# Softmax attention and a Mish feed-forward on one core: three attention outputs in a row in place of one beside each half step

## The chip, the core and the metric

The kernel runs on one core of a Trainium2 chip. A core has engines with instruction queues of their own, which run side by side and wait for one another through semaphores: TensorE (PE: matmuls, and transposes as matmuls), VectorE (DVE), ScalarE (ACT: exponentials, Mish, copies), GpSimd (POOL) and the DMA queues that SyncE (SP) and POOL feed. Each engine takes its instructions strictly in the order in which the program gives them. Matmul results land in PSUM, eight banks of 128 x 512 fp32 values; everything else on the chip lies in SBUF. The metric is the device time of one execution in microseconds.

## The reference

Attention over q, k, v of shape (8, 12, 448, 64), whose softmax has one extra term in the denominator, then a feed-forward with Mish on the (3584, 768) result:

```python
scores = scale * np.matmul(q, k.transpose(0, 1, 3, 2))
m = np.max(scores, axis=-1, keepdims=True)
e = np.exp(scores - m)
attn = e / (np.sum(e, axis=-1, keepdims=True) + np.exp(-m) + 1e-09)
x = np.matmul(attn, v)                       # -> (B*S, H*D) = (3584, 768)
h = x @ w_in                                 # (768, 2048)
g = h * np.tanh(np.log1p(np.exp(h)))         # Mish; for h > 20 the softplus is h
out = g @ w_out                              # (2048, 768)
```

Inputs and output are fp32; inside, the kernel multiplies bf16 and adds up in fp32.

## The kernel before, in words

**Pairs, units and batches.** Two heads make a pair (48 pairs, 6 to a batch), three pairs make a unit, two units a batch. The first batch (pairs 0 to 5) goes through a loop of its own. From then on the program is a loop over units u = 2 to 19 (L525): units 2 to 15 have attention, 16 to 19 are the tail with feed-forward work alone. Instructions are issued in the order of the source (`manual_schedule`, L51), so the loops are the plan of every engine's queue.

**The twelve steps of a unit (L536).** A pair has four steps. Steps 0, 1 and 2 of a pair handle two tiles of 128 query rows each; step 3 handles one and is called the half step. (A unit's steps are n = 0 to 11; 3, 7 and 11 are the half steps.) Step n does this:

- `exps` (L274): ACT takes the exponential of the scores of step n, one activation per tile, with row sums into `sums`, and so frees a scores tile.
- `flush_late` (L102): DVE makes the copies out of PSUM that were put off: of an attention output to xT (L366) or of the output product to o_sb (L422).
- Output product (`mm2_part`, L406): PE multiplies a share of the unit's pieces, of a row of products that are ready to be made for an earlier pair of batches (L456 to L471). A quarter piece is 192 columns over two of the 16 inner tiles; a unit has 56 (unit 4 has 40). `weight` (L474) says how much of it each step takes.
- `scores_ahead` (L221): PE multiplies the scores of step n + 3 into the tile just freed, and DVE takes the row maxima (L269, `negm`), which the exponential needs as its bias.

There are three scores tiles, `sc0` to `sc2`, each of two PSUM banks (L71); step n uses tile n mod 3. A half step uses only the first bank of its tile. Two more single-bank tiles, `mo0` and `mo1`, serve the output product and the in-projection in turn.

**The attention output (`av_pair`, L343).** For each pair 8 matmuls multiply the normalised, transposed exponentials eT by v; each has 64 output rows, and the two heads go to the two halves of a bank. `av_with` (L533) ties the three pairs of the unit before to the half steps of this unit: when the scores of a half step are issued, the attention output is multiplied first, into the second bank of the same scores tile (L242). Half steps are issued three steps ahead, so this falls at steps 0, 4 and 8, and each copy to xT at steps 1, 5 and 9.

**The second part of a unit (L577).** After the twelve steps come eight groups of the in-projection (`mm1_mish`, L374): 6 matmuls over the six 128-row slices of xT (L381), then Mish on ACT (L387) to gT. The third group uses the first bank of `sc0`, the others `mo` tiles. In even units these are the first eight groups of a batch and use the attention outputs that were multiplied in the same unit; in odd units they are the last eight, whose xT has been complete for a unit, while the outputs just multiplied belong to the next batch. Between the groups DVE makes the denominators (L295, L299) and normalises the exponentials (L316; the third pair on POOL, L314), SP transposes them by DMA into eT (L320), and the next unit's q and k are transposed on PE (L178), copied out (L209, L217), and its first three scores multiplied.

Of the kernel before, what the change touches and what calls it, by code (L numbers as in the profile page):

```python
# [15 lines left out]
UNIT_PAIRS = 3  # L16
# [3 lines left out]
def kernel(  # L20
# [28 lines left out]
    STEPS = 4  # L49
# [3 lines left out]
    def pool(name, bufs, space=None):  # L53
# [17 lines left out]
    sc_tiles = [  # L71
        psum.tile([128, 2, 512], FP32, tag=f"sc{i}", name=f"sc{i}") for i in range(3)
    ]
# [22 lines left out]
    ]  # L96

    loaded, casted, qkT, att, xT, gT, o_sbs, stats = {}, {}, {}, {}, {}, {}, {}, {}
    av_with = {}
    late = deque()  # L100

    def flush_late():  # L102
        while late:
            late.popleft()()

    def mo_take():

        if not mo_free:
            flush_late()
        return mo_free.popleft()  # L110
# [110 lines left out]
    def scores_ahead(limit):  # L221

        while rg["next"] < limit and rg["used"] < len(sc_tiles):
            rg["used"] += 1
            scores(rg["next"])
            rg["next"] += 1

    def scores(idx):

        p, s = divmod(idx, STEPS)  # L230
        if s == 0:
            if p < HP or p % UNIT_PAIRS == 0:
                for nm in ("negm", "sums", "expm", "den", "rden"):
                    stats[nm] = st_pool.tile([128, UNIT_PAIRS, NTILE], FP32, tag=nm, name=nm)
            at = 0 if p < HP else p % UNIT_PAIRS
            att[p] = {nm: t[:, at, :] for nm, t in stats.items()}
            att[p].update(en=en_bufs[p % N_EN], whole=dict(stats))
        st = att[p]
        qT, kT = qkT[p]
        kA, kB = kT[0:64, :], kT[64:128, :]  # L240
        sc = sc_tiles[idx % len(sc_tiles)]
        if s == STEPS - 1 and p in av_with:  # L242
            av_pair(av_with.pop(p), bank=sc[:, 1, :])
        if p >= DIAG_FROM:
            cols = tuple(range(2 * s, min(2 * s + 2, NTILE)))
            negm = st["negm"][:, cols[0] : cols[-1] + 1]
            for bk, i in enumerate(cols):
                nc.tensor.matmul(  # L248
                    sc[:, bk, 0:S], lhsT=qT[:, i].rearrange("d h r -> d (h r)"), rhs=kT,
                    start=True, stop=True,  # L250
                )
        elif s < 3:
            qa, qb = 128 * s, 64 + 128 * s
            nc.tensor.matmul(  # L254
                sc[:, 0, 0:S], lhsT=qT[0:64, qa : qa + 128], rhs=kA, start=True, stop=True
            )
            nc.tensor.matmul(
                sc[:, 1, 0:S], lhsT=qT[64:128, qb : qb + 128], rhs=kB, start=True, stop=True
            )
            cols, negm = (s, 4 + s), st["negm"][:, s : s + 5 : 4]  # L260
        else:
            nc.tensor.matmul(
                sc[0:64, 0, 0:S], lhsT=qT[0:64, 384:S], rhs=kA, start=True, stop=True
            )
            nc.tensor.matmul(
                sc[64:128, 0, 0:S], lhsT=qT[64:128, 0:64], rhs=kB, start=True, stop=True
            )
            cols, negm = (3,), st["negm"][:, 3:4]
        nc.vector.tensor_reduce(  # L269
            out=negm, in_=sc[:, 0 : len(cols), 0:S], axis=AX.X, op=ALU.max, negate=True  # L270
        )
        st["sc", s] = (sc, cols)
# [70 lines left out]
    def av_pair(p, act=False, bank=None):  # L343
        b, hp = p // HP, p % HP
        eT = att[p]["eT"]
        v_bf = casted[p][2]
        if b not in xT:
            xT[b] = xT_pool.tile([128, DM_T, S], BF16, tag="xT", name="xT")
        av = mo_take() if bank is None else bank
        for j in range(NT):  # L350
            for h in range(2):
                if p >= DIAG_FROM:
                    by_h = eT[0:SP_, j, :].rearrange("c (i h r) -> c h i r", h=2, r=64)
                    e_h = by_h[:, h]
                else:
                    e_h = eT[0:SP_, j, h * S : (h + 1) * S]
                nc.tensor.matmul(  # L357
                    av[h * 64 : (h + 1) * 64, 0:S],
                    lhsT=v_bf[:, h, j * D : (j + 1) * D],
                    rhs=e_h,  # L360
                    start=(j == 0), stop=(j == NT - 1),
                )
        copy = nc.scalar.copy if act else nc.vector.tensor_copy

        def evac():
            copy(out=xT[b][:, hp, :], in_=av[:, 0:S])  # L366
            if bank is None:
                mo_free.append(av)

        late.append(evac)  # L370
        del att[p], casted[p], qkT[p]
# [76 lines left out]
    steps = UNIT_PAIRS * STEPS  # L448
    first_mm2 = 2 * UNITS_PER_B
# [22 lines left out]


    weight = [5.2] + [1.0] * (steps - STEPS) + [0.4] * (STEPS - 1)  # L474

    LEAD = UNIT_PAIRS + 1
    LOAD_AT = (0, 3, 6)
# [47 lines left out]
    for u in range(UNITS_PER_B, N_UNITS + 2 * UNITS_PER_B):  # L525
        attn = u < N_UNITS
        filler = deque()
        for part in plan.get(u, []):
            filler.extend(mm2_part(*part))
        total, done, acc = sum(w for _, w in filler), 0, 0.0  # L530
        p0 = u * UNIT_PAIRS
        if attn and u >= first_mm2:
            av_with.update({p0 + i: p0 + i - UNIT_PAIRS for i in range(UNIT_PAIRS)})  # L533
        end = min((u + 1) * UNIT_PAIRS, N_PAIRS) * STEPS

        for n in range(steps):  # L536
            pi, s = divmod(n, STEPS)
            p, idx = p0 + pi, p0 * STEPS + n
            late_tp = u == UNITS_PER_B and n == STEPS
            if late_tp:  # L540
                transpose_pair(p0 + 2)
            exps(idx)
            if late_tp:
                evac_qk(p0 + 2)
            if u == UNITS_PER_B + 1 and n == 0:
                for j in range(2):
                    turn_on_pe(HEAD, j)
            flush_late()
            acc += weight[n]
            want = int(total * acc / sum(weight) + 1e-6)  # L550
            while done < want:
                fn, w = filler.popleft()
                fn()
                done += w
            scores_ahead(end)
            if n in LOAD_AT:
                load_pair(p0 + LOAD_AT.index(n) + LEAD)
                cast_pair(p0 + LOAD_AT.index(n) + LEAD - 1)
            early = AV_AT.get(u - UNITS_PER_B)
            if early is not None:  # L560
                if n in early:
                    av_pair(early[n])
                for pe, n0 in BY_PE.items():
                    first = 2 if pe == HEAD else 0
                    if pe // UNIT_PAIRS == u - 1 and n0 + first <= n < n0 + NT:
                        turn_on_pe(pe, n - n0)
            elif s == (2 if pi else 0) and N_PAIRS <= p < N_PAIRS + UNIT_PAIRS:
                av_pair(p - UNIT_PAIRS)
            if u - UNITS_PER_B < len(W_AT):
                load_w(W_AT[u - UNITS_PER_B].get(n, 0))  # L570
        assert done == total

        moe = u < N_UNITS + UNITS_PER_B
        b, w = (u - UNITS_PER_B) // UNITS_PER_B, u % UNITS_PER_B
        nxt = p0 + UNIT_PAIRS
        todo = sorted(range(p0, nxt), key=lambda p: p in BY_PE)
        for f in range(FF_U):  # L577
            if moe:
                mm1_mish(b, w * FF_U + f)
            if u == UNITS_PER_B and f in (2, 6) or u == UNITS_PER_B + 1 and f == 1:  # L580
                load_w(1)
            if not attn:
                continue
            if f == 0:
                denominators(att[p0]["whole"])
                normalise(todo[0], dma=todo[0] not in BY_PE)
            if f == 3:
                scores_ahead(min(nxt * STEPS + 1, N_PAIRS * STEPS))
            if f in (1, 3, 5):
                transpose_pair(nxt + f // 2, bank=f // 2 % 2)  # L590
                evac_qk(nxt + f // 2)
            if f >= FF_U - 2:
                scores_ahead(min(nxt * STEPS + f - FF_U + 4, N_PAIRS * STEPS))
            if f == 3:
                normalise(todo[1], dma=todo[1] not in BY_PE)
            if f == (4 if u >= first_mm2 else FF_U - 1):
                normalise(todo[2], dma=todo[2] not in BY_PE, on_pool=u >= first_mm2)
# [32 lines left out]
```

## Time and profile before

| | |
|---|---|
| Time, median of 3 runs | 496.76 us (494.7 to 497.88) |
| The profiled execution: span | 494.7 us (as the lowest of the runs) |
| PE: busy, matmuls | 453.2 us, 3120 |
| DVE, ACT: busy | 349.8 us, 349.1 us |
| Attention outputs of units 4 to 15 (L357 into sc) | 288 matmuls, 36 copies to xT from sc |
| Output product (L436) | 1152 matmuls |
| In-projection (L381) | 768 matmuls |
| Mean granted clock of TensorE | 0.989 |

Times in a timeline count from the start of the span. A row merges instructions that follow one another: start, length from the first's start to the last's end, engine, line, operation, output <- inputs, shapes, count, and in brackets the idle time of the engine ahead of it with what ended it. Matmuls overlap: one's end is modelled and lies behind the next one's start, so spacings are read from start to start.

### The profile page before, as it was taken

Reading aid. Unit: us, or ns where it says so; the run is one execution under the profiler, and the core shown is the slowest. Engines: PE = TensorE matmul, PEld = TensorE weight load, DVE = VectorE, ACT = ScalarE, POOL = GpSimd, SP = SyncE. Lnnn points to the kernel's source line nnn. Section 1 sums busy time; section 2 is a strip of 40 time slices with the busy share of each in tenths; the row PEclk is TensorE's granted clock in tenths of the full one; section 3 lists DMA queues with packets and bytes.
Section 4 is the critical chain, followed back from the end, with each engine's and each line's share of the span. In section 5 each row is a group of like instructions: output and inputs, shape, how many; then the busy total and the mean of one; then the engine's idle time right before and its main releaser. Section 6 shows DMA issues by size and latency. Waiting matters only on the chain.

```text
span 494.7 us, 9027 instructions
## 1 busy us (share of the span) xinstructions
PE 453.2 (92%) x3120; PEld 249.9 (51%) x3120; DVE 349.8 (71%) x706; ACT 349.1 (71%) x906; POOL 151.1 (31%) x252
## 2 busy tenths in 40 slices
PE   4466877798999999999999999999999999999996
PEld 2122433454554556555655555555555565556573
DVE  4897988788868686968878786878796878420011
ACT  5888766668787787978797878888797879502300
POOL 4622271501432424242423324242424230300000
PEclk9999997799999999999999999999999999999999
DMA  8999999979999969989998999899989696670112
GB/s 209 194 213 228 243 222 226 193 135 217 192 218 286 184 201 189 264 163 233 195 242 188 191 193 218 221 179 245 194 243 181 187 146 144 128 159 18 47 50 79
DMA packets 209453, 92.20 MB, mean 186 GB/s; under 512 B 166272, under 2 KB 205952, under 8 KB 209408
## 3 DMA queue, kind: packets, MB, share of 16 engines
q1 hardware_dynamic: 201920, 85.35, 80.7%
q0 software_dynamic: 7488, 6.29, 8.8%
q8 instruction: 24, 0.39, 0.3%
q14 instruction: 21, 0.17, 0.1%
HBM read 45.61 MB, written 11.01 MB: 114 GB/s over the span
## 4 chain that ended last, share of the span: by engine, by line
PE 72%; DVE 12%; ACT 10%; issue 2%; DMA 1%; SPq 1%; POOL 0%; DVEq 0%; ACTq 0%; POOLq 0%
PE mo L436 24%; PE mo L381 24%; ACT en L282 9%; PE sc L248 8%; DVE negm L269 6%; PE sc L357 6%; DVE en L316 3%; PE sc L381 3%; PE sc L178 3%; PE mo L357 2%; DMA k_f<-in_k_dram 1%; PE sc L254 1%; DVE xT L366 1%; PE mo L331 1%; SPq L120 1%
## 5 line engine op out<-in xcount | busy, mean ns | idle before, releaser
L282 ACT ACTIVATE en<-sc,negm 128x448 bf16<-128x448 f32 x336 | 209.2, 636 | 33.6 <-DVE negm L269 15.3
L269 DVE TENSOR_REDUCE negm<-sc 128x2 f32<-128x896 f32 x192 | 182.9, 970 | 58.4 <-PE sc L248 44.4
L436 PE MATMUL mo<-w_out_sb,gT 128*128 128x384 bf16 (+2 forms) x1152 | 167.1, 309 | 0.0
L381 PE MATMUL mo<-xT,w_in_sb 128*128 128x448 bf16 x672 | 139.8, 352 | 1.3 <-DVE xT L366 1.0
L436 PEld LDWEIGHTS <-gT 128*128 128x128 bf16 (+1 forms) x1152 | 97.3, 100 | 56.5 <-issue 5.9
L387 ACT ACTIVATE gT<-mo 128x448 bf16<-128x448 f32 x112 | 59.3, 543 | 72.6 <-PE mo L381 72.4
L381 PEld LDWEIGHTS <-w_in_sb 128*128 128x128 bf16 x768 | 72.8, 98 | 64.6 <-issue 3.7
L314 POOL TENSOR_SCALAR en<-en,rden 128x448 bf16<-128x448 bf16 x84 | 51.8, 637 | 103.4 <-DVE rden L307 69.6
L161 POOL CAST q_bf<-q_f 112x512 bf16<-112x512 f32 x47 | 28.9, 614 | 155.2 <-DMA q_f<-in_q_dram 145.8
L422 DVE COPY o_sb<-mo 128x384 f32<-128x384 f32 (+1 forms) x64 | 32.1, 502 | 60.1 <-PE mo L436 60.0
L248 PE MATMUL sc<-kT,qd 128*128 128x448 bf16 x252 | 71.7, 354 | 1.5 <-DVE qd L209 0.7
L316 DVE TENSOR_SCALAR en<-en,rden 128x448 bf16<-128x448 bf16 x252 | 69.8, 348 | 0.9
L282 ACT ACTIVATION_READ_ACCUMULATOR en<-sc,negm 128x1 f32 x336 | 69.1, 206 | 0.0
L248 PEld LDWEIGHTS <-qd 128*128 128x128 bf16 x252 | 23.5, 97 | 33.3 <-issue 16.6
L254 PE MATMUL sc<-kT,qd 64*128 64x448 bf16 x36 | 17.5, 502 | 20.4 <-ACT en L282 17.4
L357 PE MATMUL sc<-eT,v_bf 112*64 112x448 bf16 x288 | 34.0, 356 | 2.3 <-ACT en L282 1.8
L163 POOL CAST v_bf<-v_f 112x512 bf16<-112x512 f32 x48 | 29.8, 621 | 14.3 <-DMA v_f<-in_v_dram 13.4
L357 PEld LDWEIGHTS <-v_bf 112*64 112x64 bf16 x384 | 21.3, 115 | 22.8 <-issue 16.8
L162 POOL CAST k_bf<-k_f 112x512 bf16<-112x512 f32 x47 | 29.0, 617 | 5.8 <-DMA k_f<-in_k_dram 5.1
L209 DVE TENSOR_SCALAR qd<-sc 64x448 bf16<-64x448 bf16 x72 | 27.8, 386 | 0.9
L217 ACT COPY kT<-sc 128x448 bf16<-128x448 bf16 x39 | 20.8, 535 | 8.2 <-PE sc L178 8.2
L178 PEld LDWEIGHTS <-q_bf 112*128 112x128 bf16 x192 | 14.4, 104 | 16.5 <-DVE q_bf L161 4.2
(47 smaller groups left out, 275.0 us busy)
## 6 DMA issues: line engine op xcount, KB each, us to landing
q_f<-in_q_dram SPq DMA_DIRECT2D x48, 224.0 KB, 5.1
k_f<-in_k_dram SPq DMA_DIRECT2D x48, 224.0 KB, 5.2
v_f<-in_v_dram SPq DMA_DIRECT2D x48, 224.0 KB, 5.4
w_in_sb<-in_moe_w_in_dram POOLq DMA_DIRECT2D x12, 256.0 KB, 5.6
w_out_sb<-in_moe_w_out_dram POOLq DMA_DIRECT2D x8, 384.0 KB, 7.4
out_dram<-o_sb SPq DMA_DIRECT2D x7, 336.0 KB, 3.6
out_dram<-o_sb SPq DMA_DIRECT2D x8, 288.0 KB, 4.6
out_dram<-o_sb SPq DMA_DIRECT2D x8, 240.0 KB, 3.2
```

Of the source, the lines that this page charges most:

```text
L163: nc.gpsimd.tensor_copy(out=v_bf, in_=v_f)
L178: nc.tensor.transpose(by_s[s][:, t * SP_ : (t + 1) * SP_], src[:, t].rearrange("p h d -> p (h d)"), ident[:SP_, :SP_],)
L248: nc.tensor.matmul(sc[:, bk, 0:S], lhsT=qT[:, i].rearrange("d h r -> d (h r)"), rhs=kT, start=True, stop=True,)
L269: nc.vector.tensor_reduce(out=negm, in_=sc[:, 0 : len(cols), 0:S], axis=AX.X, op=ALU.max, negate=True)
L282: nc.scalar.activation(out=st["en"][:, :, c, 0:SP_], in_=sc[:, bk, 0:S].rearrange("q (j c) -> q j c", j=NT), func=AF.Exp, bias=st["negm"][ ...
L314: nc.gpsimd.tensor_scalar(scalar2=1.0, op0=ALU.mult, op1=ALU.mult, **args)
L316: nc.vector.tensor_scalar(scalar2=None, op0=ALU.mult, **args)
L357: nc.tensor.matmul(av[h * 64 : (h + 1) * 64, 0:S], lhsT=v_bf[:, h, j * D : (j + 1) * D], rhs=e_h, start=(j == 0), stop=(j == NT - 1),)
L381: nc.tensor.matmul(h_ps[:, 0:S], lhsT=w_in_sb[:, dm, ff * 128 : (ff + 1) * 128], rhs=xT[b][:, dm, :], start=(dm == 0), stop=(dm == DM_T - 1),)
L387: nc.scalar.activation(out=gT[b][:, ff, :], in_=h_ps[:, 0:S], func=AF.Mish)
L422: nc.vector.tensor_copy(out=o_sb[:, cols], in_=st["o"][:, 0:n_cols])
L436: nc.tensor.matmul(st["o"][r : r + n, 0:n_cols], lhsT=gT[bb][:, ff, c0 : c0 + n], rhs=w_out_sb[:, ff, cols], start=(ff == 0), stop=(ff == ...
```

## The change

The attention outputs are no longer tied to half steps. In units 4 to 15, at step 10 (`steps - 2`), behind that step's exponentials and after all scores and product pieces of the unit, the three outputs are multiplied in a row: into both banks of `sc0`, whose last exponentials in the unit are those of step 9, and into the second bank of `sc2`, whose first bank still holds the scores of step 11. Their copies to xT are made by the `flush_late` of step 11. For these units the output product is dealt by new weights, `weight_av`: more at step 0, somewhat more in steps 1 to 8, none in the last three. The other units keep `weight`, and the tail keeps its own outputs (L567).

```diff
@@ in scores
         sc = sc_tiles[idx % len(sc_tiles)]
-        if s == STEPS - 1 and p in av_with:
-            av_pair(av_with.pop(p), bank=sc[:, 1, :])
@@
     weight = [5.2] + [1.0] * (steps - STEPS) + [0.4] * (STEPS - 1)
+    weight_av = [7.0] + [1.25] * (steps - STEPS) + [0.0] * (STEPS - 1)
@@ in the loop over units
-        if attn and u >= first_mm2:
-            av_with.update({p0 + i: p0 + i - UNIT_PAIRS for i in range(UNIT_PAIRS)})
+        grouped = attn and u >= first_mm2
+        share = weight_av if grouped else weight
@@ in the loop over steps
-            acc += weight[n]
-            want = int(total * acc / sum(weight) + 1e-6)
+            acc += share[n]
+            want = int(total * acc / sum(share) + 1e-6)
             while done < want:
                 fn, w = filler.popleft()
                 fn()
                 done += w
             scores_ahead(end)
+            if grouped and n == steps - 2:
+                free = (sc_tiles[0][:, 0, :], sc_tiles[0][:, 1, :], sc_tiles[2][:, 1, :])
+                for i, bank in enumerate(free):
+                    av_pair(p0 + i - UNIT_PAIRS, bank=bank)
```

More of the change, by code (lines that the diff above doesn't have):

```diff
@@ L98 @@
     loaded, casted, qkT, att, xT, gT, o_sbs, stats = {}, {}, {}, {}, {}, {}, {}, {}
-    av_with = {}
     late = deque()
```

## The prediction, made before the changed kernel was run

> **What bounds the kernel now.** The page first: busy shares and the chain that ended last.
>
> ```profile
> PE 453.2 (92%) x3120; PEld 249.9 (51%) x3120; DVE 349.8 (71%) x706; ACT 349.1 (71%) x906; POOL 151.1 (31%) x252
> ...
> PE 72%; DVE 12%; ACT 10%; issue 2%; DMA 1%; SPq 1%; POOL 0%; DVEq 0%; ACTq 0%; POOLq 0%
> ```
>
> TensorE (PE) carries the end, ScalarE (ACT) and VectorE (DVE) little of it. A busy PE is not PE at its peak, so I read spacings, in the timeline of unit 12 (an even unit), PE alone. Columns: start, length in us, engine, line, operation, count.
>
> ```profile
> 324.87 3.41 PE L436 MATMUL mo<-w_out_sb,gT 128*128 128x384 bf16 x20
> ...
> 328.21 0.95 PE L357 MATMUL sc<-eT,v_bf 112*64 112x448 bf16 x8
> 329.09 0.36 PE L248 MATMUL sc<-kT,qd 128*128 128x448 bf16 x1
> 329.29 0.81 PE L436 MATMUL mo<-w_out_sb,gT 128*128 128x384 bf16 x4
> 329.94 0.54 PE L248 MATMUL sc<-kT,qd 128*128 128x448 bf16 x2
> 330.32 0.81 PE L436 MATMUL mo<-w_out_sb,gT 128*128 128x384 bf16 x4
> 330.97 0.54 PE L248 MATMUL sc<-kT,qd 128*128 128x448 bf16 x2
> ...
> 338.07 0.95 PE L357 MATMUL sc<-eT,v_bf 112*64 112x448 bf16 x8
> ...
> 339.98 2.43 PE L381 MATMUL mo<-xT,w_in_sb 128*128 128x448 bf16 x12
> ```
>
> Start to start, four output-product matmuls take 0.65 (0.1625 each), two scores 0.38, a half step's one 0.19. Call T0 the start of the unit's output product (324.87) and S the start of its first in-projection matmul (L381, 339.98): S - T0 = 15.11 us. PE's rows fill that: 56 quarter pieces x 0.1625 = 9.10, scores 6 x 0.38 + 3 x 0.19 = 2.85, three attention outputs (below) x 0.98 = 2.94: 14.89, so 0.2 of waiting. From S to the next T0 (351.38) are 11.40 us; 48 in-projections x 0.19, three transpose groups x 0.39 and six scores x 0.19 make 11.43. So PE is full in both halves, and what is lost ahead of S is not made good behind it.
>
> ACT in the same unit, and who waited for the attention output's copy (L366: us, times):
>
> ```profile
> 326.55 0.63 ACT L282 ACTIVATE en<-sc,negm 128x448 bf16<-128x448 f32 x1
> ...
> 330.83 0.63 ACT L282 ACTIVATE en<-sc,negm 128x448 bf16<-128x448 f32 x1 [0.49 <-DVE xT L366]
> ```
> ```profile
>   ACT en L282: 9.6, 24
> ```
>
> The first exponentials start at T0 + 1.68 and follow at 0.61 each. The half step's exponential reads the first bank of its scores tile and waited 0.49 for a copy (330.10 to 330.71) that reads only the second bank of that tile. So accesses to one tile are ordered even where the banks differ. This decides much below.
>
> **The change, part by part.**
>
> *Attention outputs out of the half steps.* One is 8 matmuls, in pairs: starts 328.21, 328.42, 328.61, 328.80, and the next scores at 329.09. The product's last start ahead was 327.95, so it ended at 328.11: 0.10 of gap, 0.88 of work and gap, 0.98 in all. Three in a row have one gap at each end: 3 x 0.765 + 0.20 = 2.50 in place of 2.94. By itself, 0.44 a unit less on PE, 12 units (4 to 15): -5.3 us.
>
> The Trainium skill says the same in "TensorEngine Tiling (Array Packing)", Key Properties: changing the tiling mode drains the engine. The 0.10 us gaps agree; by that rule alone the change would give -5.3 us.
>
> *Output product dealt anew.* Of 56 pieces step 0 takes 24 (before 20), steps 1 to 8 four each as before, and the last three steps none (before four in all). Nothing is added; but ahead of the attention outputs PE now has no work that waits for nobody.
>
> *The new wait.* In program order PE has, after the last scores (step 8), the three outputs, then the in-projection. The first output takes tile 0 and needs both exponentials of step 9 done. Before, PE did product pieces and two in-projection groups (2.27 us) there, while ACT finished steps 9 to 11. So I work out when step 9 ends, in us from T0, with the latencies of these rows: scores start to reduction 0.47 for one bank and 0.58 for two; reductions 0.53 and 1.04 apart, the latter 1.08 long; 0.06 to the exponential; 0.14 from an exponential's end to PE (337.93 to 338.07).
>
> ACT: step 0 at 1.68, step 1 at 2.90, step 2 at 4.12, free at 5.34. PE: 24 pieces to 3.90, scores 3 at 3.90, reduction 4.37 to 4.9, step 3 at 5.34, no wait: the copy that it waited for is gone. ACT is free at 5.95. Scores 4 at 3.90 + 0.19 + 0.65 = 4.74; reduction 5.32 to 6.40; step 4 at 6.45: 0.5 of idle ACT. From here ACT (3 x 1.22 + 0.61 = 4.27 for four steps) is slower than PE (3 x 1.03 + 0.84 = 3.93) and DVE (3 x 1.04 + 0.53 + one product copy 0.53 = 4.18), so it sets the pace but for small waits where a product copy falls between reductions (0.17, 0.05): step 5 at 7.67, 6 at 9.06, 7 at 10.28, 8 at 10.89, 9 at 12.16. Step 9 ends at 12.16 + 0.61 + 0.63 = 13.40; PE has done all else by 12.7. Outputs from 13.54 to 15.84, S at 15.94, against 15.11: **+0.83**. The same recurrence with the old order gives 15.16 here and 15.01 for odd units (measured 14.95 in unit 15), so it is good to 0.1. Odd units: 15.94 against 15.01, **+0.93**. Units 6, 10 and 14, whose product begins with 64-row pieces, have a measured 15.67 (unit 14); the recurrence gives +0.82. Unit 4 has only 40 pieces and took 14.95 (110.13 to 125.08); ACT starts at T0 + 1.50, and 18 exponentials, 0.14 and the outputs' 2.4 make 15.0; with the small waits 15.2, +0.25.
>
> *Copies.* Three L366 copies now follow one another at step 11 (0.53 apart), in the same number. The third output goes to tile 2's second bank, while step 11 is still to read the first. If one tile's accesses are ordered, as above, then step 11's exponential waits for the third output (15.84 + 0.3), ends at 16.8, and the third copy waits for it: 16.94 to 17.55. In even units the in-projection uses these rows: its sixth matmul needs the third copy. (In the trace the first five go ahead: at 97.69 they began before a copy that ran from 97.80.) It could start at 15.94 + 0.95 = 16.89 and starts at 17.65: **+0.75**, six even units. In odd units the in-projection reads the other batch, so 0.
>
> Queued behind that third copy on DVE are the denominators, the normalisation and the next pair's scaled q. They end at 17.55 + 3.1 = 20.65; scores for the next unit wait for the q, and PE comes there at S + 4.93 = 20.87: covered, with 0.2 to spare, so at most 0.1 here. Table load and Mish: the tile that the fourth in-projection group needs is free at step 11's end + 2.2 = 19.0, PE comes at S + 3.8 = 19.74: covered. The eT tiles are held longer, to step 10; the next transposes are issued at 343.98 here, some 4 us behind S: covered. SP's and POOL's queues get the same instructions in the same order.
>
> **Sum.** Unit 4: 0.25 + 0.75 = 1.0. Units 8 and 12: 2 x 1.58 = 3.2. Units 6, 10, 14: 3 x 1.57 = 4.7. Six odd: 6 x 0.93 = 5.6. Together +14.5; I take +13.8, since such a recurrence runs up to 0.06 a unit high. Against the profiled span of 494.7 that is 508.5; the span is the lowest of the three runs (494.7), and the median is 2.06 above it. Against the median 496.76: **510.5 us**, +2.8%.
>
> **Rivals.**
>
> *Banks are told apart.* Then step 11 doesn't wait for the third output, the third copy ends at about 16.7, in time for the sixth matmul, and 6 x 0.75 = 4.5 us go: 506. For it: outputs in two banks of one tile. Against: the 0.49 us wait above, 24 such waits. The Trainium skill ("PSUM — Partial Sum Buffer", section on bank collisions) has different banks accessed at once run clean, so the chip would need no wait; whether this program takes that freedom is what the 0.49 us row denies. Chance 0.15.
>
> *ACT never waits.* Step 9 then ends at 1.68 + 18 x 0.61 = 12.66; S at 15.2: +0.25 odd, +0.1 and -0.45 in the two kinds of even units, still +0.75 there: 1.5 + 1.7 + 0.9 + 1.0 = +5, 502. For it: the x-copies leave DVE's middle. Against: 24 pieces ahead of scores 3. Chance 0.10.
>
> *Faster.* PE stays the bound and keeps the saved gaps, -5.3 us: 491.5. It decides at step 9 ending by T0 + 11.8 (9.10 + 2.85 less 0.14), where PE would arrive unhindered. Against: 18 exponentials at 0.61 after 1.68 make 12.66, and a table load (1.28) stands ahead of the 1.68. Chance 0.04.
>
> *Exponentials go no faster.* If step 9 ends as late as before (14.4 to 14.5), S is 17.0: +2 a unit and the 0.75: +26, 523. It needs DVE as late without the copies as with them. Chance 0.08.
>
> **Numbers.** The forecast has 0.63 (own range 507 to 515). Slower by over 1%: 0.63 + 0.15 + 0.08 + half of the third = 0.90; within 1%: 0.06; faster: 0.04. One per cent is about what a measurement tells from no change (the runs differ by 0.6%). The range, 502.5 to 516, takes in both milder rivals and 0.45 a unit beyond the forecast.
>
> **What would show it.** S - T0 near 15.9; an idle PE ahead of the first L357, put down to ACT L282, 0.6 to 0.9 us a unit; step 11 waiting for PE L357 over 1 us; in even units the in-projection's sixth matmul waiting for xT L366 about 0.7; the three outputs 2.3 to 2.5 us from first to last. Wrong it would be if step 9 ended before T0 + 12.8, if PE stalled less than 0.3 at the outputs, or if the half S to T0 shrank below 11.3.

## The result, and the profile after

The changed kernel takes 508.67 us (median of 5 runs, 506.74 to 509.46) against 496.76 us: a ratio of 1.0234, with a 95% interval of 1.0207 to 1.026. Forecast were 510.5 us and +2.8%.

The page of the changed kernel, busy shares and the chain that ended last:

```profile
PE 453.7 (89%) x3120; PEld 256.6 (51%) x3120; DVE 348.8 (69%) x706; ACT 348.7 (69%) x906; POOL 151.2 (30%) x252
...
PE 60%; ACT 18%; DVE 12%; DMA 6%; issue 3%; SPq 1%; POOL 0%; DVEq 0%; POOLq 0%
```

The span is 507.7 us, 13.0 more, and the engines are busy as long as before (PE 453.7 against 453.2; only PEld, which overlaps PE, shows 6.7 more): no work was added, so the time is waiting. PE's share of the chain fell from 72% to 60%, ACT's rose from 10% to 18%. DMA's rise from 1% to 6% is not the change: the chain's transfers all end by 87 us, ahead of unit 4, where both kernels run the same program. (Line numbers have moved by 3: L436 is L433 here, L381 L378, L357 L354, L282 L279, L366 L363, L269 L266, L248 L245.)

Unit 12 again, PE alone in the timeline of the changed kernel:

```profile
333.30 4.06 PE L433 MATMUL mo<-w_out_sb,gT 128*128 128x384 bf16 x24
337.20 0.35 PE L245 MATMUL sc<-kT,qd 128*128 128x448 bf16 x1
...
345.77 0.35 PE L245 MATMUL sc<-kT,qd 128*128 128x448 bf16 x1
346.86 2.46 PE L354 MATMUL sc<-eT,v_bf 112*64 112x448 bf16 x24 [0.74 <-ACT en L279]
349.26 1.12 PE L378 MATMUL mo<-xT,w_in_sb 128*128 128x448 bf16 x5
350.80 1.48 PE L378 MATMUL mo<-xT,w_in_sb 128*128 128x448 bf16 x7 [0.42 <-DVE xT L363]
```

T0 is 333.30, S is 349.26: S - T0 = 15.96 us, against 15.11 before. The last scores go out at T0 + 12.47, then PE has nothing to do until ACT is through with step 9, and the three outputs begin at T0 + 13.56. Behind them five matmuls of the in-projection run, and the sixth (350.80, where 350.21 would have been in step) waits for the third copy.

ACT and DVE in the same unit:

```profile
334.98 0.63 ACT L279 ACTIVATE en<-sc,negm 128x448 bf16<-128x448 f32 x1
...
339.82 0.63 ACT L279 ACTIVATE en<-sc,negm 128x448 bf16<-128x448 f32 x1 [0.41 <-DVE negm L266]
...
349.36 0.64 ACT L279 ACTIVATE en<-sc,negm 128x448 bf16<-128x448 f32 x1 [1.09 <-PE sc L354]
```
```profile
348.68 1.16 DVE L363 CAST xT<-sc 128x448 bf16<-128x448 f32 x2 [0.98 <-PE sc L354]
350.12 0.62 DVE L363 CAST xT<-sc 128x448 bf16<-128x448 f32 x1 [0.29 <-ACT en L279]
```

The first row is step 0, the second step 4 (late, since 24 product pieces stand ahead of the scores of step 3), the third step 11: it waits 1.09 us for the third output, which writes the other bank of its tile. The third copy then waits for step 11. The first copy waits for the second output too, though its own bank was done 0.76 us earlier: the two share `sc0`. What the attention outputs waited for and, further down the same answer, who waited for them (us, times):

```profile
  ACT en L279: 9.3, 12
...
  ACT en L279: 14.7, 12
```

Both come once in each of the twelve units.

**Unit by unit.** S - T0 is the stretch from a unit's first product piece to its first in-projection matmul; the second half runs from there to the next T0, read from PE's timeline. The length of units 4 to 15 (T0 of unit 4 to T0 of unit 16) leaves out the start, which differs by up to 3.3 us from run to run.

| us | before | changed |
|---|---|---|
| S - T0, odd units 7 to 15 | 14.95 to 14.96 | 15.95 |
| S - T0, units 8, 12 | 15.10, 15.11 | 15.95, 15.96 |
| S - T0, units 6, 10, 14 | 15.67 to 15.68 | 16.54 to 16.55 |
| S - T0, unit 4 | 14.95 | 15.55 |
| second half, even units 6 to 14 | 11.40 to 11.41 | 11.99 to 12.00 |
| second half, odd units 7 to 13 | 11.56 to 11.66 | 11.41 to 11.51 |
| second half, unit 5 | 12.62 | 11.51 |
| units 4 to 15 | 319.18 | 331.23 |

The difference, 12.05 us, is the whole loss (the medians differ by 11.9): in S - T0 10.9, in the even units' second halves 3.2 (unit 4's, 11.81 and 12.00, among them), less 2.0 in the odd units'. The rest of the span's 13.0 is 0.94 ahead of unit 4, where the program is the same.

### The profile page after: what moved, and what is told of

Read it like the earlier page. It is cut to its first block, busy times and chain, and to the rows that moved or that the text cites. A ratio compares the mean times of both kernels' runs of the same rounds, so it can differ in the third digit from the quotient of the medians.

```text
span 507.7 us, 8987 instructions
## 1 busy us (share of the span) xinstructions
PE 453.7 (89%) x3120; PEld 256.6 (51%) x3120; DVE 348.8 (69%) x706; ACT 348.7 (69%) x906; POOL 151.2 (30%) x252
## 4 chain that ended last, share of the span: by engine, by line
PE 60%; ACT 18%; DVE 12%; DMA 6%; issue 3%; SPq 1%; POOL 0%; DVEq 0%; POOLq 0%
PE mo L378 23%; ACT en L279 17%; PE mo L433 17%; DVE negm L266 6%; PE sc L354 6%; PE sc L245 4%; PE sc L378 3%; DMA eT<-en 3%; PE sc L177 3%; DVE en L313 2%; PE mo L354 2%; DMA k_f<-in_k_dram 1%; DMA q_f<-in_q_dram 1%; DVE o_sb L419 1%; DVE xT L363 1%
## 5 line engine op out<-in xcount | busy, mean ns | idle before, releaser
L279 ACT ACTIVATE en<-sc,negm 128x448 bf16<-128x448 f32 x336 | 209.2, 639 | 39.6 <-DVE negm L266 15.6
L266 DVE TENSOR_REDUCE negm<-sc 128x2 f32<-128x896 f32 x192 | 181.9, 971 | 60.7 <-PE sc L245 45.1
L433 PE MATMUL mo<-w_out_sb,gT 128*128 128x384 bf16 (+2 forms) x1152 | 165.0, 309 | 0.0
L378 PE MATMUL mo<-xT,w_in_sb 128*128 128x448 bf16 x672 | 139.9, 353 | 2.8 <-DVE xT L363 2.8
L433 PEld LDWEIGHTS <-gT 128*128 128x128 bf16 (+1 forms) x1152 | 97.3, 100 | 58.9 <-issue 5.4
L378 PEld LDWEIGHTS <-w_in_sb 128*128 128x128 bf16 x768 | 71.8, 98 | 69.5 <-issue 9.7
L245 PE MATMUL sc<-kT,qd 128*128 128x448 bf16 x252 | 71.2, 352 | 5.4 <-ACT en L279 3.9
L279 ACT ACTIVATION_READ_ACCUMULATOR en<-sc,negm 128x1 f32 x336 | 70.3, 209 | 0.0
L313 DVE TENSOR_SCALAR en<-en,rden 128x448 bf16<-128x448 bf16 x252 | 67.9, 342 | 0.9
L354 PEld LDWEIGHTS <-v_bf 112*64 112x64 bf16 x384 | 25.7, 116 | 27.3 <-issue 18.6
L245 PEld LDWEIGHTS <-qd 128*128 128x128 bf16 x252 | 23.9, 98 | 28.6 <-issue 12.6
L354 PE MATMUL sc<-eT,v_bf 112*64 112x448 bf16 x288 | 29.5, 353 | 9.3 <-ACT en L279 9.3
L363 DVE CAST xT<-sc 128x448 bf16<-128x448 f32 x36 | 21.4, 622 | 17.1 <-PE sc L354 13.6
```

The source lines that it names most:

```text
L245: nc.tensor.matmul(sc[:, bk, 0:S], lhsT=qT[:, i].rearrange("d h r -> d (h r)"), rhs=kT, start=True, stop=True,)
L266: nc.vector.tensor_reduce(out=negm, in_=sc[:, 0 : len(cols), 0:S], axis=AX.X, op=ALU.max, negate=True)
L279: nc.scalar.activation(out=st["en"][:, :, c, 0:SP_], in_=sc[:, bk, 0:S].rearrange("q (j c) -> q j c", j=NT), func=AF.Exp, bias=st["negm"][ ...
L313: nc.vector.tensor_scalar(scalar2=None, op0=ALU.mult, **args)
L354: nc.tensor.matmul(av[h * 64 : (h + 1) * 64, 0:S], lhsT=v_bf[:, h, j * D : (j + 1) * D], rhs=e_h, start=(j == 0), stop=(j == NT - 1),)
L378: nc.tensor.matmul(h_ps[:, 0:S], lhsT=w_in_sb[:, dm, ff * 128 : (ff + 1) * 128], rhs=xT[b][:, dm, :], start=(dm == 0), stop=(dm == DM_T - 1),)
```

## The experiments

Theory A is that of the prediction: the loss is PE's wait for step 9, and the chain of third output, step 11, third copy, sixth matmul, which follows from the order of accesses to one tile. Theory B: the new deal of the output product costs the time, since it takes away the pieces that lay beside the last exponentials. Rival C holds that step 11 waits for PE for some other reason. All ratios are to the kernel before, measured beside each run.

| | median us | ratio, 95% interval | units 4 to 15, us |
|---|---|---|---|
| changed kernel | 508.67 | 1.0234 (1.0207 to 1.026) | 331.23 |
| old deal, outputs in a row | 509.64 | 1.0297 (1.0231 to 1.0363) | 333.52 |
| new deal, outputs at half steps | 510.20 | 1.0274 (1.0226 to 1.0321) | 333.21 |
| third output in an mo tile | 505.48 | 1.0187 (1.0149 to 1.0225) | 328.90 |
| first output in an mo tile, others in sc0 | 498.61 | 1.0053 (1.003 to 1.0077) | 321.71 |
| two chunks behind the outputs | 510.83 | 1.0286 (1.0257 to 1.0314) | 334.81 |
| two chunks between the outputs | 516.84 | 1.0411 (1.0374 to 1.0447) | 340.59 |
| first and third in mo tiles, product dealt evenly | 494.52 | 0.9952 (0.9929 to 0.9976) | 316.84 |

### The old deal with the outputs in a row

```diff
-        share = weight_av if grouped else weight
+        share = weight
```

> The changed kernel with the old shares of the output product (5.2, 1.0, 0.4) in all units. Theory A (the loss is PE's wait for step 9 ahead of the three outputs, and in even units the wait for the third copy): the place of the outputs is unchanged, so most of the loss stays. Fewer pieces at step 0 let step 9 end some 0.5 us earlier in even units, but one to two pieces now lie behind the outputs: S - T0 about 15.7 in units 8 and 12, 16.3 in odd units, the even units' wait for the third copy down from 0.6 to about 0.3; together 507 to 510 us. Theory B (the new deal costs the time, since it takes the pieces away that hid the end of the exponentials): back to 497 to 500.

Measured: 509.64 us; S - T0 is 16.28 to 16.29 in odd units, 15.83 to 15.84 in units 8 and 12, and the even units' second half 11.73, so a wait of 0.33 is left there. These are the expected sizes, and the 497 to 500 us of theory B are not reached. A cost that was not foreseen lies in the odd units: their second half is 11.93 to 12.03, 0.5 above that of the changed kernel. PE in unit 13:

```profile
376.25 0.50 PE L433 MATMUL mo<-w_out_sb,gT 128*128 128x384 bf16 x2
376.58 1.30 PE L378 MATMUL mo<-xT,w_in_sb 128*128 128x448 bf16 x6
378.25 1.30 PE L378 MATMUL mo<-xT,w_in_sb 128*128 128x448 bf16 x6 [0.37 <-DVE o_sb L419]
```

The last product pieces now stand behind the outputs, their copy on DVE behind the three copies to xT, and the second in-projection group needs the tile that this copy frees.

### The new deal with the outputs at the half steps

```diff
+    weight_av = [7.0] + [1.25] * (steps - STEPS) + [0.0] * (STEPS - 1)
...
+        share = weight_av if attn and u >= first_mm2 else weight
...
-            acc += weight[n]
+            acc += share[n]
```

> The kernel before, its outputs still at the half steps, with the new shares of the output product in units 4 to 15. Theory A: PE stays near full; odd units lose about 1 us, since step 0 holds the scores of step 3 back by 24 pieces and an output and nothing is left for the end, even units gain 0.2 to 0.4; together 499 to 503 us. Theory B (the new deal is the loss): 507 to 510.

Measured: 510.20 us, theory B's number; A's expectation missed it. Its terms for S - T0 held (odd units 15.88, +0.92; units 8 and 12 14.93, -0.18; units 6, 10, 14 15.27, -0.41), but it had said nothing on what comes behind S: all second halves are 0.8 to 1.2 longer (even units 12.30, units 4 and 12 about 12.6, odd 12.50 to 12.59), apart from unit 5 (+0.34). ACT's row for step 11 of unit 13, then PE's rows of that unit, whose S is 377.83 (lines as in the kernel before):

```profile
379.81 0.63 ACT L282 ACTIVATE en<-sc,negm 128x448 bf16<-128x448 f32 x1 [0.66 <-DVE xT L366]
```
```profile
377.83 2.71 PE L381 MATMUL mo<-xT,w_in_sb 128*128 128x448 bf16 x12
380.59 0.36 PE L178 MATMUL sc<-ident,q_bf 112*128 112x112 bf16 x4
...
382.55 1.29 PE L381 MATMUL mo<-xT,w_in_sb 128*128 128x448 bf16 x6 [0.28 <-ACT gT L387]
```

Step 11 ends at S + 2.6; in the kernel before it ended at S + 1.5 (unit 13: 367.20 + 0.63 against 366.33). The transposes behind the second group begin at 380.59, not at S + 2.27 = 380.10: the second group itself starts 0.27 late, at 379.24, since the product copy that frees its tile ended only at 379.19, and the transposes then wait 0.22 for step 11's tile. The fourth group waits for a Mish that stands behind step 11 and the table load. So PE gets to S 0.9 late in odd units and a little early in even ones, but ACT is later still, and PE then waits in the second half.

ACT's waits for copies of the outputs, like the one in the first row, come to 27.5 us in this run (35 times), against 9.6 (24 times) in the kernel before: here too a half step's exponential waits for a copy out of the other bank of its tile, and in unit 13 a product copy now stands ahead of that copy on DVE. How much of the 14.0 us that this run loses over units 4 to 15 is this, and how much the missing pieces, no run separates.

Together the two runs say that the losses of the two parts do not add up: either part alone costs at least as much as both. The new deal leaves PE without work that waits for nobody near the end of the exponentials; with the outputs at the half steps PE then runs ahead of ACT into the second half, with the outputs in a row it waits at step 9. Theory B is refuted as the sole cause, and A is incomplete in not pricing the deal where the exponentials end.

### The third output in another tile

```diff
-                free = (sc_tiles[0][:, 0, :], sc_tiles[0][:, 1, :], sc_tiles[2][:, 1, :])
+                free = (sc_tiles[0][:, 0, :], sc_tiles[0][:, 1, :], None)
```

(`None` takes an mo tile, which is free by then.)

> The changed kernel with the third output in a free mo tile in place of the second bank of sc2. Theory A (accesses to one tile are ordered though the banks differ): step 11's exponential no longer waits for the third output (it starts some 1.1 us earlier) and the third copy no longer waits for it; the copy then follows the other two at once and ends some 0.3 us earlier, so the even units' second half falls from 12.0 to about 11.7 us; odd units stay; 506 to 508 us. Rival C (step 11 waits for PE for another reason, or the chip holds it): step 11 still waits about 1.1 us ahead of its exponential, and the time is that of the changed kernel, 508 to 509.

Measured: 505.48 us, half a microsecond below the expected 506 to 508; over units 4 to 15 the run is 2.3 us shorter than the changed kernel. The even units' second half is 11.61 to 11.62 (expected about 11.7), S - T0 and the odd units' halves stay within 0.1. ACT's step 11 in unit 12, and DVE's third copy:

```profile
344.10 0.63 ACT L279 ACTIVATE en<-sc,negm 128x448 bf16<-128x448 f32 x1
```
```profile
345.67 0.61 DVE L363 CAST xT<-mo 128x448 bf16<-128x448 f32 x1
```

Step 11 follows step 10 without a gap, beside the third output (344.30 to 345.18) that held it up in the changed kernel, and no wait of ACT for an attention output is left. Rival C is refuted: it was the shared tile. What is left of the even units' wait, 0.2 us, is the row of three copies.

### The first output in another tile, so that PE need not wait for step 9

```diff
-                free = (sc_tiles[0][:, 0, :], sc_tiles[0][:, 1, :], sc_tiles[2][:, 1, :])
+                free = (None, sc_tiles[0][:, 0, :], sc_tiles[0][:, 1, :])
```

> The changed kernel with the first output in a free mo tile, the second and third in the two banks of sc0, so that only the second waits for step 9, when the first is done. Theory A: PE's idle time of 0.75 us ahead of the outputs goes in all 12 units, S - T0 falls from 15.95 to about 15.2, and step 11 is free of PE; the even units' wait for the third copy stays at 0.3 to 0.5; 497 to 500 us. Theory B or any cause apart from the wait for step 9: 506 or more.

Measured: 498.61 us, 1.0053 of the kernel before. PE in unit 12 (T0 is 325.42):

```profile
337.89 0.35 PE L245 MATMUL sc<-kT,qd 128*128 128x448 bf16 x1
338.17 0.95 PE L354 MATMUL mo<-eT,v_bf 112*64 112x448 bf16 x8
338.98 1.70 PE L354 MATMUL sc<-eT,v_bf 112*64 112x448 bf16 x16
340.61 1.20 PE L378 MATMUL mo<-xT,w_in_sb 128*128 128x448 bf16 x5
342.00 1.49 PE L378 MATMUL mo<-xT,w_in_sb 128*128 128x448 bf16 x7 [0.18 <-DVE xT L363]
```

The outputs follow the last scores at once, and S - T0 is 15.18 to 15.20 in odd units and units 8 and 12, as expected; the even units keep 0.44 (11.84), since the second and third copy both wait for the end of the third output, which shares `sc0` with the second (DVE waits 0.45 us for it, until 340.79). Of the 12.05 us lost, 9.5 come back, with the grouping and the new deal untouched. The edit moves all three outputs, so it frees step 11 as well; but 9.15 of the 9.5 lie in S - T0, ahead of step 11, where the wait for step 9 (9.3 us in the changed kernel) is what went. The even units' second halves give 0.95, and the odd ones take back 0.6. This is the largest part of theory A, shown by itself.

S - T0 is still 0.24 above that of the kernel before in odd units, though PE's own work there is 0.44 less (9.10 + 2.85 + 2.50 = 14.45): PE now waits some 0.7 us a unit ahead of its last scores, since ACT sets the pace.

### What a change of tiling costs

Two runs hold back the last two product chunks of a unit and put them behind the outputs, or one each behind the first and the second output:

```diff
+        hold = [filler.pop(), filler.pop()] if attn and u >= first_mm2 else []
+        total -= sum(w for _, w in hold)
...
                 for i, bank in enumerate(free):
                     av_pair(p0 + i - UNIT_PAIRS, bank=bank)
+                    if hold:
+                        hold.pop()[0]()
```

This is the run with the chunks between; with the chunks behind, `while hold` stands after the loop.

> The changed kernel with the last two product chunks of each unit of 4 to 15 held back and multiplied right behind the three outputs, as the measure for the run with the chunks between the outputs. Theory A (a change of the array's tiling costs 0.10 us each way): S - T0 in odd units about 16.25 (outputs from 13.3, 2.4 for them, 0.65 for the two chunks), the even units' wait for the third copy down to about 0.3; 508 to 511 us. If pieces behind the outputs simply fill idle time, 503 to 506.

> The same two chunks, one behind the first output and one behind the second: same work, two round trips more between the tilings. Theory A: S - T0 of every unit 0.4 us above that with the chunks behind (odd units about 16.65), 4.8 us in all, and the even units wait for the third copy in full again, another 0.3 in six units; 513 to 518 us. Rival (the gaps of 0.10 us belong to the wait for tiles, not to the change of tiling): S - T0 the same as with the chunks behind within 0.1, and at most 2 us between the two runs.

PE in unit 13, chunks behind, then chunks between:

```profile
374.33 2.46 PE L354 MATMUL sc<-eT,v_bf 112*64 112x448 bf16 x24 [0.99 <-ACT en L279]
376.72 0.82 PE L433 MATMUL mo<-w_out_sb,gT 128*128 128x384 bf16 x4
377.38 2.64 PE L378 MATMUL mo<-xT,w_in_sb 128*128 128x448 bf16 x12
```
```profile
380.06 0.95 PE L354 MATMUL sc<-eT,v_bf 112*64 112x448 bf16 x8 [0.99 <-ACT en L279]
380.94 0.50 PE L433 MATMUL mo<-w_out_sb,gT 128*128 128x384 bf16 x2
381.38 0.95 PE L354 MATMUL sc<-eT,v_bf 112*64 112x448 bf16 x8
382.25 0.50 PE L433 MATMUL mo<-w_out_sb,gT 128*128 128x384 bf16 x2
382.68 0.95 PE L354 MATMUL sc<-eT,v_bf 112*64 112x448 bf16 x8
383.56 2.44 PE L378 MATMUL mo<-xT,w_in_sb 128*128 128x448 bf16 x12
```

Outputs and chunks take 3.05 us from first to last in the one (374.33 to 377.38) and 3.50 in the other (380.06 to 383.56), with the same matmuls. S - T0 differs by 0.44 in every unit: four changes of tiling at 0.11 us. That is the price read from the gaps before, now by itself; the rival (a wait for tiles) foresaw no difference and is out. The two runs are 6.0 us apart by their medians and 5.8 over units 4 to 15, where 6.6 was expected: S - T0 adds 5.3, the even units wait in full again in the second (12.00 against 11.73, 1.6 in all), but the odd units' second half is shorter there (11.51 against 11.70, 1.2 in all), since in program order the product's last copy comes ahead of the third copy to xT. The level of S - T0 missed (16.95 in odd units, about 16.65 expected), as it did with the chunks behind.

The rule that the Trainium skill states in "TensorEngine Tiling (Array Packing)", Key Properties, that a change of tiling mode drains the engine, agrees with these 0.11 us. That it goes by the columns, and not by the 112 rows that these matmuls also have, the transposes show: they are 112x128 and follow the in-projection without a gap (in unit 12 of the kernel before at 342.25, twelve matmuls of 0.19 behind 339.98).

One expectation of the run with the chunks behind failed in part: the outputs were to begin at T0 + 13.3, and began at 13.45 (374.33 - 360.88), so S - T0 was 16.51 and not 16.25. Four pieces fewer ahead of step 9 did not bring it forward by what was put down; and 13.3 + 2.4 + 0.65 is 16.35, so 0.1 was a slip of the sum.

### A version without the waits, and the product dealt for it

```diff
-    weight_av = [7.0] + [1.25] * (steps - STEPS) + [0.0] * (STEPS - 1)
+    weight_av = [
+        [n0] + [(56 - n0) / 8] * (steps - STEPS) + [0.0] * (STEPS - 1) for n0 in (18.0, 20.0)
+    ]
...
-        share = weight_av if grouped else weight
+        share = weight_av[u % 2] if grouped else weight
...
-                free = (sc_tiles[0][:, 0, :], sc_tiles[0][:, 1, :], sc_tiles[2][:, 1, :])
+                free = (None, sc_tiles[0][:, 0, :], None)
```

> The changed kernel with the first and third output in the mo tiles and the second in sc0, and the product dealt with 18 pieces (even units) or 20 (odd units) at step 0 and the rest evenly over steps 1 to 8: a try for a version as fast as the kernel before or faster. Theory A: the outputs no longer wait for step 9 nor the third copy for step 11, and ACT no longer waits for the scores of step 4; S - T0 about 15.1 in odd units and units 8 and 12, 15.5 in units 6, 10, 14; second halves 11.4 to 11.5; 493 to 496 us, even with the kernel before or up to 0.6% faster. Theory B (grouping itself costs): 500 or more.

Measured: 494.52 us (11 runs, 492.06 to 495.87), 0.9952 of the kernel before (0.9929 to 0.9976): the fastest of all, faster than before by 0.5%. PE in unit 13 (T0 is 351.01):

```profile
359.93 0.54 PE L245 MATMUL sc<-kT,qd 128*128 128x448 bf16 x2 [0.21 <-ACT en L279]
...
363.34 0.35 PE L245 MATMUL sc<-kT,qd 128*128 128x448 bf16 x1
363.62 0.95 PE L354 MATMUL mo<-eT,v_bf 112*64 112x448 bf16 x8
364.44 0.95 PE L354 MATMUL sc<-eT,v_bf 112*64 112x448 bf16 x8
365.20 0.95 PE L354 MATMUL mo<-eT,v_bf 112*64 112x448 bf16 x8
366.08 2.44 PE L378 MATMUL mo<-xT,w_in_sb 128*128 128x448 bf16 x12
```

S - T0 is 15.07 to 15.08 in odd units, 15.12 in units 8 and 12, 15.33 to 15.54 in units 6, 10 and 14, and every second half is 11.41 to 11.51, PE's own sum. These are the expected sizes, so the waits are gone and the loss with them. The gain, though, is not the drains'. Summed over the twelve units S - T0 is 181.9 us, as in the kernel before: the 0.44 a unit saved is taken up by PE's waits for scores tiles that ACT frees (the first row; 15.07 in odd units against 14.45 of work). The 2.3 us gained over units 4 to 15 (316.84 against 319.18) all lie in the second halves, 2.0 of them in the odd units, where the changed kernel gained as much. Whether outputs in a row are worth having by themselves is therefore not shown; a run with the outputs at the half steps in tiles of their own, and the product ended as early, would be needed.

## Why the prediction was right

The forecast was +13.8 us by the place of each wait; the twelve units lost 12.05 and the medians differ by 11.9. The waits came where they were put. That the total came so near is in part luck: against the sum of 14.5, S - T0 lost 0.9 more than worked out (10.9 against 9.95), the even units' second halves 1.3 less (3.2 against 4.5), and the odd ones gained 2.0 that the sum did not have. The 0.7 taken off because the recurrence runs high has no support in the result: it ran low in every kind of unit.

- **Step 9.** Worked out: outputs from T0 + 13.54, S at 15.94 in unit 12. Measured: 13.56 and 15.96. By kind of unit +0.93, +0.83, +0.82 were forecast, and +1.00, +0.85, +0.87 measured. The run with the first output in an mo tile removes this wait and nothing else ahead of S, and S - T0 falls to 15.2 in odd units and units 8 and 12.
- **The pause at step 4.** Forecast 0.5, measured 0.41 (339.82). As forecast, ACT then sets the pace.
- **One tile, two banks.** The step read it from a 0.49 us wait of the kernel before. It held: 1.09 us at step 11, 14.7 in twelve units, and gone with the third output in another tile. The rival that banks are told apart (0.15) is out. The Trainium skill ("PSUM — Partial Sum Buffer", bank collisions) lets different banks be accessed at once; the run with the third output in an mo tile shows the two side by side, so it was the order that the program keeps within a tile that held step 11.
- **The third copy in even units.** +0.75 forecast, +0.60 measured: the term was a quarter too large, since step 11 followed the third output sooner than the 0.3 us put down (it began at 349.36, 0.2 behind the outputs' end at 346.86 + 2.30).
- **Attention outputs in a row.** 2.50 us with both gaps forecast; from first start to S 2.40, with the first gap hidden in the wait. The price of a drain, 0.10, measured 0.11 in the pair of runs above.
- **Unit 4.** +0.25 and +0.75 forecast, +0.60 and +0.19 measured: 0.2 less in sum, with both terms off. Step 9 ended at T0 + 13.0 (124.09, by a row of small waits), not 12.5; and the second half of the kernel before (11.81) already held 0.4 of other waits, which the new one covers (12.00, as in the other even units).
- **Odd units' second half.** Here the step failed: "in odd units the in-projection reads the other batch, so 0", and at most +0.1 for the next unit's scores. Measured: -0.14 to -0.24 a unit, and -1.11 in unit 5. The second in-projection group needs the mo tile of the last product pieces, and before it waited for their copy. The first row of unit 5 of the kernel before shows it:

```profile
153.49 1.29 PE L381 MATMUL mo<-xT,w_in_sb 128*128 128x448 bf16 x6 [0.35 <-DVE o_sb L422]
...
157.89 0.55 PE L248 MATMUL sc<-kT,qd 128*128 128x448 bf16 x2 [0.44 <-DVE qd L209]
```

  The new deal ends the product at step 8, so that this copy is long done. A step that is moved earlier frees its tile earlier, and this term was left out. It is not the whole 2.0 us, though. In unit 5 the wait for the copy is 0.51 of the 1.11 (153.49, where 152.98 would have been in step). The other 0.60 is the second row, a wait for the next pair's scaled q, which stood on DVE behind a normalisation of 2.66 us; in the changed kernel this took 1.81. Why is open. The new deal alone does not settle it: the run with the first output in an mo tile has that deal, and waits at this place in unit 5 again (0.30, second half 11.98). So the copy accounts for at most 1.4 us.
- **The span and the runs.** The prediction took the profiled execution for the lowest of the three runs, since both read 494.7. In the runs that list both, the time is 1.8 us above the span (507.7 and 509.46), so a span of 494.7 belongs to a time near the median of 496.76, and not to the lowest run. As the sum was added to the median, nothing hangs on it.
- **The rivals.** "Exponentials go no faster" (step 9 at 14.4) and "ACT never waits" (12.66) enclose the measured 13.4; "faster" needed step 9 by T0 + 11.8. (In the chances, 0.63, 0.15, 0.08 and half of 0.10 make 0.91, where 0.90 stands, and the rival at 0.10 is the second, not the third.)

## What to carry to other kernels

Work that waits for nobody, standing in front of the last link of a slower engine's chain, hides that engine's end: before a product is dealt anew, ask when the slower engine's last item ends against the point where PE will need it, and carry that distance through the next stage too. Here the new deal alone cost 14.0 us over units 4 to 15, waits for shared tiles among them, where the drains were to save 5.3. Before results are put into the free half of a buffer, see whether the program orders accesses by the whole buffer: a wait between operations on different banks in the trace is the sign, and another buffer, where one is free, removes it. And when a mended version comes out faster, see in which stretch: the last run's gain lies in the second halves, not in the stretch that grouping was to shorten.

## What the runs showed of the hardware

A change of TensorE between 128-column and 64-column tiles costs 0.11 us each way in this kernel: 0.44 us for four, the same in every unit. Eight 64-column matmuls of 448 columns take 0.76 us in a row (364.44 to 365.20 in the last run, start to start), the time of four 128-column ones at 0.19: the two heads' matmuls run side by side. ACT and PE work on different PSUM tiles side by side with no visible loss: step 11's exponential took 0.63 us beside the third output as alone (344.10 in the run with the third output in an mo tile).
